# One DMA queue with a four-slot ring, and output weights cut by partitions, in a cached-attention decode kernel

## The chip, the core and the metric

The kernel runs on one core of one Trainium2 chip. The metric is the device time of one execution in microseconds (us), measured on the chip. The core has five engines with instruction streams of their own: TensorE (PE), VectorE (DVE), ScalarE (ACT), GpSimd (POOL) and SyncE (SP). Transfers from memory to the on-chip buffer (128 partitions) are issued by SP or ACT, each into its own hardware queue, and are carried out by 16 DMA engines that both queues share.

## What is computed

One decode step for four sequences: layer norm, attention over a cache, output projection and residual, then layer norm, a gated block and a second residual.

```python
def _A_ref(x, k_cache, v_cache, wq, wo):          # B=4, Sq=1, D=512, H=32, Sk=8192, Dh=128
    q = (x @ wq).reshape(B, Sq, H, Dh).transpose(0, 2, 1, 3)
    scores = jnp.einsum("bhqd,bhkd->bhqk", q, k_cache) * (Dh ** -0.5)
    p = _softmax(scores, axis=-1)
    o = jnp.einsum("bhqk,bhkd->bhqd", p, v_cache)
    return o.transpose(0, 2, 1, 3).reshape(B, Sq, H * Dh) @ wo

def _B_ref(x, w_gate, w_up, w_down):              # F=1792
    g = jnp.einsum("bsd,df->bsf", x, w_gate)
    u = jnp.einsum("bsd,df->bsf", x, w_up)
    return jnp.einsum("bsf,fd->bsd", _sigmoid(g) * u, w_down)

h  = x + _A_ref(_layernorm(x), k_cache, v_cache, wq, wo)
h2 = h + _B_ref(_layernorm(h), w_gate, w_up, w_down)
```

All data are bf16. The two caches are 268 MB each, so nearly everything that the kernel reads is keys and values.

## The kernel before

**Tiles.** The 128 pairs of sequence and head are the steps s. Two heads make one tile t of 4 MB: `ring[:, slot, :]`, 128 partitions with 32 KB each. There are 64 key tiles and 64 value tiles. The ring has NS = 4 slots. `place` (L179 to L189) gives the slots: key tile t has slot t % 2, value tile t has slot 2 + t % 2. The query weights (`wq`) begin in slot 3, and slot 2 first holds the re-ordered queries ("qr"). After the attention slot 0 takes the gate and up weights, slot 1 the down weights.

**A step.** VectorE transposes half a key tile into `kT` with four instructions (L389), TensorE multiplies it by the queries (L407). Every eight steps (GS = 8, a group) the maximum is taken (L445 to L462), ScalarE applies the exponential (L466, L468), the probabilities are transposed (L484) and copied (L498). LAG = 10 steps after its scores a step's values are used (`pe_pv`, L431): in program order TensorE runs score(s), then P·V(s − 10). Each group of results is scaled (L503), transposed (L510) and kept in `OT` (L515).

**What sets the order of loads.** `P(engine, ...)` appends an instruction to that engine's list; each engine works its list in order, and an instruction with dependencies makes its engine wait. Loads are such instructions. SP issues wq, all 64 key tiles, then gate, up and down weights (L251, L252). ACT issues x (L202), value tiles 0 and 1 once the queries are in place (L521, L522), and each further value tile t in the main loop, right after the P·V that uses up tile t − 2, between its own exponentials and copies. A load waits until the tile that was in its slot is used up: for keys its last transpose, for values its last P·V (`consumed`). Gate, up and down weights wait also for P·V of step 123 (`pv_of[NST - 5]`).

**Output weights.** `wo` (4 MB, 32 heads × 128 rows × 512) lands in the space of `kT`, so its loads wait for the last score (`sc_of[NST - 1]`). They are eight transfers of all 128 partitions × 4 heads, 512 KB each, in contiguous pieces of 1 KB (L209), issued by ACT between the value tiles 61, 62 and 63 (`wo_after`). The last value tile comes in three pieces (`VL_PARTS`, L217), the down weights in three parts (`WD_PARTS`, L225).

**The end.** After all output weights have landed TensorE multiplies those of 24 heads (L578), then the P·V of the last value tile follows piece by piece, its scaling, the output projection's rest (L578), the residual and layer norm (L598 to L615), gate and up (L624), sigmoid and product (L629, L630), down (L638), the second residual (L644), a transposition (L647, L649) and the store (L653).

## Time and profile before

| | us |
|---|---|
| three timed runs | 1314.25, 1317.78 (median), 1319.87 |
| the profiled execution | 1314.25 |
| its span, first to last instruction | 1312.3 |
| VectorE busy | 625.6 (48%) |
| TensorE matmuls busy | 473.4 (36%) |
| ScalarE busy | 46.0 (4%) |
| SP's queue (q1) | 278.14 MB, 49.6% of 16 engines' time |
| ACT's queue (q10) | 272.64 MB, 48.7% |
| key tile, issue to landing | 29.6 |
| value tile, issue to landing | 32.2 |
| one part of the output weights | 18.8 |

A row of groups on the page gives line, engine and operation, output from input, shape and count, then busy time, mean duration in ns, idle time of that engine just before them and what ended it. The chain of waits follows the work that ended last back to its releaser at each step; in it "ACTq L209" is time in which ACT's sequencer was busy issuing the DMA of line 209. Slices are fortieths of the span, 32.8 us each. Windows are stretches of our choice with the busy time of every engine.

The packet records behind the page list every packet of every DMA with its queue, size, start and duration. Their medians are: 32 KB (one partition of a key or value tile) 1215 ns, 16 KB 618 ns, 8 KB 315 ns, 3.5 KB (gate and up weights) 147 ns, 1 KB (output and down weights) 47 ns. Each transfer of 128 partitions also has 16 packets of 4 B, its completions.

### The profile page before, as it was taken

To read this page: it belongs to the slowest core of one execution; us is meant where nothing else is said; L and a number is where in the kernel's file an instruction comes from. 1 tells how busy PE (TensorE), PEld (TensorE's weight loads), DVE (VectorE), ACT (ScalarE), POOL (GpSimd) and SP (SyncE) were. 2 spreads that over 40 slices of the span, in tenths; PEclk is the share of its full clock that TensorE was granted. 3 is DMA by queue.
4 is the path that set the end of the run, shared out by engine and by line. 5 is a ranking of instruction groups with operands and counts; after the bars stand their busy time and mean duration, and the time that the engine had idled before them with its cause. 6 is when DMAs were issued, how large, how long until landed. Compare 5 with 4: busy or idle time off the path is not lost.

```text
span 1312.3 us, 12694 instructions
## 1 busy us (share of the span) xinstructions
PE 473.4 (36%) x5827; PEld 176.8 (13%) x5827; DVE 625.6 (48%) x641; ACT 46.0 (4%) x102; POOL 10.6 (1%) x22
## 2 busy tenths in 40 slices
PE   2134342333333253332334244243243234323324
PEld 1011110111111010110111011011111111111113
DVE  5486455445355355445446445445535436545300
ACT  2000000000000000000000000000000000000000
POOL 3000000000000000000000000000000000000000
PEclk9997556775566656676665655676556665577665
DMA  9999999999999999999999999999999999999895
GB/s 402 432 380 418 434 430 432 430 431 429 430 432 430 431 430 432 431 430 431 429 431 432 431 431 432 431 430 432 428 432 431 430 430 431 431 430 430 356 396 209
DMA packets 26076, 551.58 MB, mean 420 GB/s; under 512 B 2340, under 2 KB 8232, under 8 KB 9256
## 3 DMA queue, kind: packets, MB, share of 16 engines
q1 hardware_dynamic: 12288, 278.14, 49.6%
q10 hardware_dynamic: 13736, 272.64, 48.7%
q8 instruction: 45, 0.74, 0.2%
q14 instruction: 7, 0.06, 0.0%
HBM read 550.77 MB, written 0.00 MB: 420 GB/s over the span
## 4 chain that ended last, share of the span: by engine, by line
DMA 71%; DVE 24%; ACTq 3%; PE 1%; issue 1%; ACT 0%; DVEq 0%
DMA ring<-in_A_k_cache_dram 66%; DVE kT L389 22%; DMA ring<-in_A_v_cache_dram 3%; ACTq L209 2%; DMA ring<-in_A_wq_dram 1%; ACTq L217 1%; DVE mx L445 1%; ACTq L245 0%; PE PS L322 0%; DVE Lq L366 0%; DVE rowx L457 0%; PE PS L624 0%; PE PS L431 0%; DVE mrow L455 0%; DVE ring L339 0%
## 5 line engine op out<-in xcount | busy, mean ns | idle before, releaser
L389 DVE STREAM_TRANSPOSE kT<-ring 128x1024 uint32<-128x1024 uint32 x512 | 588.2, 1209 | 591.1 <-DMA ring<-in_A_k_cache_dram 591.1
L407 PE MATMUL PS<-kT,Lq 128*32 128x512 bf16 x2048 | 217.6, 566 | 773.5 <-DVE kT L389 606.5
L431 PE MATMUL PS<-ring,PTz 128*32 128x512 bf16 x2048 | 210.1, 553 | 33.9 <-DMA ring<-in_A_v_cache_dram 33.6
L407 PEld LDWEIGHTS PS<-kT,Lq 128*32 128x32 bf16 x2048 | 53.9, 119 | 914.8 <-DVE kT L389 673.0
L431 PEld LDWEIGHTS PS<-ring,PTz 128*32 128x32 bf16 x2048 | 64.8, 125 | 132.8 <-issue 81.0
L466 ACT ACTIVATE negm<-PS 128x1 f32<-128x1 f32 x16 | 2.7, 171 | 1157.2 <-PE PS L462 1157.2
L503 DVE TENSOR_SCALAR Zs<-PS,rinv 128x512 f32<-128x512 f32 x16 | 11.6, 724 | 49.4 <-PE PS L431 49.4
L498 ACT ACTIVATE PTz<-PS 64x512 bf16<-64x512 f32 x32 | 18.9, 591 | 18.5 <-PE PS L484 18.1
L510 PE MATMUL PS<-SelZ,Zs 128*128 128x8 f32 x128 | 18.2, 269 | 0.9 <-DVE Zs L503 0.9
L510 PEld LDWEIGHTS PS<-SelZ,Zs 128*128 128x128 f32 x128 | 16.7, 204 | 10.2 <-issue 8.4
L484 PEld LDWEIGHTS PS<-Sel,E_sb 128*32 128x32 bf16 x1024 | 11.3, 100 | 9.1 <-ACT E_sb L468 6.7
L484 PE MATMUL PS<-Sel,E_sb 128*32 128x32 bf16 x1024 | 11.4, 188 | 1.5 <-ACT E_sb L468 1.1
L445 DVE TENSOR_REDUCE mx<-PS 128x1 f32<-128x512 f32 x16 | 10.5, 657 | 1.3 <-PE PS L407 1.2
L468 ACT ACTIVATE E_sb<-PS,negm 128x512 bf16<-128x512 f32 x16 | 11.0, 687 | 0.5
L473 PEld LDWEIGHTS PS<-sig,Gsum 128*128 128x128 f32 x32 | 7.8, 305 | 12.6 <-issue 12.6
L515 DVE CAST OT<-PS 128x8 bf16<-128x8 f32 x16 | 2.1, 132 | 15.5 <-PE PS L510 15.5
L473 PE MATMUL PS<-sig,Gsum 128*128 128x1 f32 x32 | 9.2, 356 | 0.0
L578 PE MATMUL PS<-OT,kT 128*128 128x4 bf16 (+2 forms) x160 | 4.6, 167 | 11.3 <-DMA kT<-in_A_wo_dram 11.0
L462 PE MATMUL PS<-onesf,rowx 1*128 1x1 f32 x32 | 7.5, 300 | 0.0
L462 PEld LDWEIGHTS PS<-onesf,rowx 1*128 1x128 f32 x32 | 6.1, 237 | 9.8 <-issue 9.8
L339 DVE CAST ring<-PS 128x512 bf16<-128x512 f32 x4 | 2.5, 684 | 9.8 <-PE PS L322 9.8
L578 PEld LDWEIGHTS PS<-OT,kT 128*128 128x128 bf16 x160 | 4.4, 103 | 12.2 <-issue 11.9
(78 smaller groups left out, 77.1 us busy)
## 6 DMA issues: line engine op xcount, KB each, us to landing
ring<-in_A_k_cache_dram SPq DMA_DIRECT2D x64, 4096.0 KB, 29.6
ring<-in_A_v_cache_dram ACTq DMA_DIRECT2D x63, 4096.0 KB, 32.2
ring<-in_A_wq_dram SPq DMA_DIRECT2D x1, 4096.0 KB, 12.2
kT<-in_A_wo_dram ACTq DMA_DIRECT2D x8, 512.0 KB, 18.8
ring<-in_A_v_cache_dram ACTq DMA_DIRECT2D x1, 2048.0 KB, 28.3
ring<-in_A_v_cache_dram ACTq DMA_DIRECT2D x2, 1024.0 KB, 21.8
ring<-in_B_w_gate_dram SPq DMA_DIRECT2D x1, 1792.0 KB, 16.2
ring<-in_B_w_up_dram SPq DMA_DIRECT2D x1, 1792.0 KB, 21.8
```

The lines of the kernel that those rows point to most:

```text
L209: return [(lambda e: e.dma_start(wo_v[:, HW * t:HW * t + HW, :], A_wo.rearrange("(h p) f -> p h f", p=128)[:, HW * t:HW * t + HW, :]).then ...
L217: return e.dma_start(ringv(slot)[:, c0:c1], kv_src(t, A_v_cache)[:, c0:c1]).then_inc(s_piece[i], 16)
L389: return e.transpose(kT[:, buf, i * q:(i + 1) * q].bitcast(U32), ringv(src)[:, base + i * q:base + (i + 1) * q].bitcast(U32))
L407: mm = e.matmul(bS[g % 2][32 * j:32 * (j + 1), :], Lq[:, l0:l0 + 32], rhs, start=(s % GS == 0 and v == 0), stop=(s % GS == GS - 1 and v == 3),
L431: mm = e.matmul(bO[g % 2][32 * rq:32 * (rq + 1), :], PTz[:, g % 2, l0:l0 + 32], ringv(slot)[:, r0 * 128:(r0 + 4) * 128], start=(s % GS == ...
L445: mx_of[g] = P("dve", lambda e: e.tensor_reduce(mx[:, :], bS[g % 2][:, :], AX.X, ALU.max), [sc_of[g * GS + GS - 1], p1_of.get(g - 1)])
L462: p2_of[g] = P("pe", lambda e: e.matmul(bX[:, 0:1], rowx[0:1, :], onesf[0:1, 0:1], start=True, stop=True), [d2b_of[g], c_ones])
L473: L_of[g] = P("pe", lambda e: e.matmul(bX[:, 0:1], Gsum[:, :], sig[:, 0:1], start=True, stop=True), [exp_of[g], a1_of[g], d_g])
L484: mm = e.matmul(bP[g % 2][32 * a:32 * (a + 1), 32 * rr:32 * rr + 32], E_sb[:, 32 * rr:32 * rr + 32], Sel[:, a, :], start=True, stop=True, ...
L498: return e.activation(dst, src, ACT.Copy)
L503: z_of[g] = P("dve", lambda e: e.tensor_scalar(Zs[:, :], bO[g % 2][:, :], rinv[:, g % 2:g % 2 + 1], None, op0=ALU.mult), [pv_of[g * GS + G ...
L510: mm = e.matmul(bX[:, 256:264], Zs[:, 128 * r:128 * (r + 1)], SelZ[:, r, :], start=(r == 0), stop=(r == 3))
```

## The change

All loads but that of x are issued by SP, in one order: wq, key tiles 0 to 4, then alternately key t and value t − 5, the last five value tiles, and gate, up and down weights. The four slots are given in turn to every load in that order, instead of two to keys and two to values. The output weights stand after value 60 (two transfers), after value 61 (five) and after value 62 (three). They are ten transfers instead of eight: four of partitions 0 to 79 with eight heads each (640 KB), and six of eight partitions each (80 to 87, and so on to 127) with all 32 heads (256 KB). All still wait for the last score. The extra wait of gate, up and down weights goes. The compute instructions and their order stay, except that "qr" moves from slot 2 to slot 3.

```diff
-        NWO = 8
-        HW = H // NWO
...
-        place(("wq", 0), 3)
-        for t in range(NT2):
-            place(("k", t), t % 2)
-            place(("v", t), 2 + t % 2)
-        place(("wg", 0), 0)
-        slot_of[("wu", 0)], prev_of[("wu", 0)] = 0, prev_of[("wg", 0)]
-        place(("wd", 0), 1)
+        WO_PARTS = [(0, 80, 8 * i, 8 * i + 8) for i in range(4)] + [(p, p + 8, 0, H) for p in range(80, 128, 8)]
+        NWO = len(WO_PARTS)
+        LAG2 = LAG // 2
+        items = [("wq", 0)]
+        for t in range(NT2 + LAG2):
+            if t < NT2:
+                items.append(("k", t))
+            if t >= LAG2:
+                items.append(("v", t - LAG2))
+            for i in {LAG2 - 4: (0, 1), LAG2 - 3: (2, 3, 4, 5, 6), LAG2 - 2: (7, 8, 9)}.get(t - NT2, ()):
+                items.append(("wo", i))
+        items += [("wg", 0), ("wu", 0), ("wd", 0)]
+        slot_of, prev_of, dma_of = {}, {}, {}
+        owner = [None] * (NS - 1) + [("qr", 0)]
+        uses = [0] * NS
+        cur = 0
+        for it in items:
+            if it[0] == "wo":
+                continue
+            if it[0] == "wu":
+                slot_of[it], prev_of[it] = slot_of[("wg", 0)], prev_of[("wg", 0)]
+                continue
+            slot_of[it] = cur
+            prev_of[it] = [owner[cur]] if owner[cur] is not None else []
+            owner[cur] = it
+            cur = (cur + 1) % NS
...
             if kind == "wo":
+                p0, p1, h0, h1 = WO_PARTS[t]
                 return [(lambda e: e.dma_start(
-                    wo_v[:, HW * t:HW * t + HW, :],
-                    A_wo.rearrange("(h p) f -> p h f", p=128)[:, HW * t:HW * t + HW, :]).then_inc(s_wo, 16),
+                    wo_v[p0:p1, h0:h1, :],
+                    A_wo.rearrange("(h p) f -> p h f", p=128)[p0:p1, h0:h1, :]).then_inc(s_wo, 16),
                     s_wo, 16 * NWO)]
...
-        for it in [("wq", 0)] + [("k", t) for t in range(NT2)] + [("wg", 0), ("wu", 0), ("wd", 0)]:
-            issue("sp", it)
+        for it in items:
+            dma_of[it] = [P("sp", fn, (), sem, val) for fn, sem, val in load(it)]
...
-        issue("act", ("v", 0))
-        issue("act", ("v", 1))
-        wo_after = {NT2 - 3: (0, 1), NT2 - 2: (2, 3, 4), NT2 - 1: (5, 6, 7)}
...
-            t = (s - LAG - 1) // 2 + 2
-            if (s - LAG) % 2 == 1 and 2 <= t < NT2:
-                for i in wo_after.get(t, ()):
-                    issue("act", ("wo", i))
-                issue("act", ("v", t))
...
-        for it, ops in dma_of.items():
-            for op in ops:
+        for it in items:
+            for op in dma_of[it]:
                 op.deps = [sc_of[NST - 1]] if it[0] == "wo" else [consumed[p] for p in prev_of[it]]
-                if it[0] in ("wg", "wu", "wd"):
-                    op.deps.append(pv_of[NST - 5])
```

## Prediction

> **What bounds the kernel now.** I read the page's slices first, then the DMA windows where the slices dip, then the chain of waits at the end.

> ```profile
> span 1312.3 us, 12694 instructions
> ...
> DMA  9999999999999999999999999999999999999895
> GB/s 402 432 380 418 434 430 432 430 431 429 430 432 430 431 430 432 431 430 431 429 431 432 431 431 432 431 430 432 428 432 431 430 430 431 431 430 430 356 396 209
> DMA packets 26076, 551.58 MB, mean 420 GB/s; under 512 B 2340, under 2 KB 8232, under 8 KB 9256
> ```

> From slice 4 to 36 the rate sits at 428 to 434 GB/s with the DMA engines busy throughout, while VectorE, the busiest compute engine, works 48% of the span. The middle is bound by bytes. In the timeline the first transposes of successive key tiles start at 1140.73, 1160.16, 1179.59 and 1199.01: 19.43 us for one key and one value tile, so 9.715 us per 4 MB tile. Only the dips can be won: slices 2, 3 and the last three.

> The windows of 10 us over the first dip (columns: busy time of each engine, clock, DMA share, GB/s):

> ```profile
> 80.00:90.00 10.00, 4.10 (x33) 0.98 (x33) 9.40 (x10) 0.00 (x0) 0.00 (x0) 1.00 0.86 338
> 90.00:100.00 10.00, 4.55 (x98) 2.00 (x98) 8.69 (x10) 2.13 (x5) 0.00 (x0) 1.00 0.91 367
> 100.00:110.00 10.00, 5.36 (x58) 1.83 (x50) 7.00 (x8) 0.00 (x0) 0.00 (x0) 0.89 0.98 398
> ```

> Here both value slots are full and the values' use begins ten half-tiles after the keys' (LAG). Only keys flow, through two slots; the next load waits for eight transposes (9.13 us), and DMA runs dry in between. Against 432 the five windows from 60 to 110 lose 5.4 us.

> The last lines of the chain of waits (start, length, what):

> ```profile
> 1262.66 10.18 ACTq L217
> 1272.84 0.03 issue
> 1272.87 1.41 ACTq L217
> 1274.28 0.03 issue
> 1274.31 22.60 DMA ring<-in_A_v_cache_dram
> 1296.92 0.04 issue
> 1296.96 1.07 PE PS L431 x5
> ```

> The last value pieces are issued late from ACT, behind the output weights, and land while gate, up and down weights arrive on the other queue. After 1296.96 DMA has nothing left and 15.3 us of compute follow alone. A third hole is around 1220 to 1240: value tile 60 is issued at 1229.9, when tile 58 has been used, and the two windows there run at 234 and 389 GB/s, 5.6 us lost.

> **The change, part by part.**

> *One queue, four slots in turn.* Sixty-four key loads, all value loads and the output weights now stand on SP in one order. Is one queue as fast as two? From 10 to 20 us, before the first value is issued (22.57), SP's queue alone moved 436 GB/s, and the packet records show ACT's alone at 432 GB/s from 1246 to 1252. So no loss per tile; bound 0 to 0.03 us, over 125 tiles under 4 us.

> SP now stops at each slot wait and everything behind it stops too. A load waits for the use of the tile four loads earlier. A key tile is used up 9.13 to 10.6 us after landing; three more tiles (29.1 us) stand between it and its successor, so 18 us stay queued. A value tile is used about 5 us after landing (score, 1.9 us, and P·V, 1.9 us, twice, behind the key's second half), leaving 24 us. The tightest spots: key 2 waits for the query transposition (done at 21.15; key 1 keeps DMA busy to 32), the first value behind key 5 waits for key 2's transposes (53; DMA is busy to 71). Output weights wait for the last score, some 3 us after value 58 lands, with values 59 and 60 (19 us) queued. All hidden; if a cover failed, the cost is one issue-to-data gap of about 2 us.

> ACT loses 74 issues. Its longest wait row, 1157.2 us for the max, is slack, so this is worth nothing by itself.

> The start is no longer starved: keys 0 to 5 flow at 9.715 us each, transposes with their chain steps need about 10 us, three slots of lead take the difference. The first tile (query weights) lands at 12.9 as now. Then 64 keys and values 0 to 60 are 125 tiles × 9.715 = 1214.4, so value 60 lands at 1227.3.

> *The end.* Behind it in the same queue: values 61 to 63, 3 × 9.715 = 29.1; output weights 4096 packets of 1 KB at 47 ns over 16 engines, 12.0; gate and up 1024 × 147 ns / 16 = 9.4; down 1792 × 47 ns / 16 = 5.3. DMA would end at 1283.1 if all were spread evenly. The last values now land 14.7 us before that end. From there to the normalized row is 7.5 us (1296.96 to 1304.42), gate/up 3.2, sigmoid and product 0.3: 11.0, beside the remaining 14.7, with 3.7 us of cover. What stays after DMA is landing 0.3, the last two sevenths of L638 (1.67 → 0.5) and from its end 1309.65 to 1312.3, 2.65. Together 3.4 and **1286.5**: 25.8 below now. The places seen add up to 5.4 + 5.6 + (15.3 − 3.4) = 22.9; 3 us of that gain I cannot place.

> *The output weights' new shapes.* Four transfers of 80 rows × 8 heads, then six of 8 rows × 32 heads. How many engines take a transfer is visible in the small packets: 146 transfers, 145 of them with 16 completion packets make 2320, the result's 16 pieces of 256 B make 2336, and the 2340 of the page leave 4 for the load of x, which has four rows. Transfers of 80 = 16 × 5 rows should then use 16 engines, 4 × 40 × 47 ns = 7.5 us. An 8-row transfer should use 8, each with 32 packets: the loads of the other 8 engines do not help. Engines drain in order, so the loaded half ends last, and everything after it in its queue is late.

> Its price c is not in the trace. Lower end: eight engines run free of each other, 32 × 47 ns = 1.5 us; the nearest row is x, whose four packets to four neighbouring partitions took 44, 44, 44 and (the first) 506 ns, two of them at the same time. Upper end: eight partitions take no more than the one engine that feeds eight partitions of every 4 MB tile, 256 KB in 9.7 us. On the same grounds the 80-row transfers cost up to 2.4 us in place of 1.9, 2.2 in all. The end is at 1286.5 − 12.0 + 7.5 + 6c = **1282.0 + 6c**: 1291.0 at the lower end, 1340.2 at the upper. x is one packet per engine and shows no sustained rate; the tile shows one, but never several engines upon the same partitions. Neither is like 32 packets from each of eight engines, so I take the middle, c = 5.6, and 1315.6.

> [...]

> *Scale.* The profiled execution took 1314.25 for a span of 1312.3, 1.95 around it; the median of the three runs, 1317.78, is 3.5 above it. I add both: 1315.6 + 5.5 = **1321**.

> **The rivals.** A measurement of this kernel can tell about 0.5%, 6.6 us, from no change; the limits are 1311.2 and 1324.4. By 1282.0 + 6c they lie at c = 3.95 and 6.15, and the balance at 5.05.

> 1. Forecast: the gain of one full queue is eaten by the eight-row transfers, c about 5.6 (4.0 to 6.1): 1311 to 1324. Chance 0.42.
> 2. The eight engines do not hinder each other, or the transfers are spread over all 16 and so do nothing: 1296.5, or 1292 when even. For it: x's overlapping packets, and that the hole-free queue is then all that counts. Against: x is 4 KB. With prices between, up to c = 3.9: 1292 to 1311. Chance 0.28.
> 3. Slower: eight neighbouring partitions are fed at little more than one engine's 27 GB/s, from c = 6.15 on, up to 1345.7. For it: no eight partitions are ever filled faster in the trace. Against: that rate is the engine's own, 32 KB in 1.215 us. Value 62's load, which stands between the two groups of three, then competes for the same partitions and lengthens both. Chance 0.25.
> 4. The one queue stalls at a slot: if each of 64 pairs lost 0.5 us (the 60 to 110 stretch lost 5.4 us on some four keys), 32 us, 1353 with c = 5.6. The backlog of 18 us speaks against it. Chance 0.05.

> **How the numbers follow.** Faster is case 2, 0.28; within 0.5% is case 1, 0.42; slower is 3 and 4, 0.30. The likeliest is 1321, its own range 1311 to 1324. For 8 in 10 I go from 1293, taking in case 2 nearly whole, to 1337, which is c = 8.25; beyond that I leave about 0.1, and 0.03 below.

> **What would show it.** Right on the queue: slices 2 and 3 at 428 or more, one hardware queue with nearly all the packets, pairs still 19.43 us apart, value 60 landing near 1227. Right on the end: the last load to land is the down weights', some 3.4 us before the end. Right on c: between the landing of value 61 and the first part of value 63 the rate falls to about half or less for some 30 us, and the six transfers take about 34 us of it. The forecast is wrong if that stretch stays above 300 GB/s (case 2), if it lasts over 37 us (case 3), or if SP's waits show DMA idle in the middle (case 4).

## The result, and the profile after

The changed kernel takes 1332.19 us (median of four runs, 1329.23 to 1333.36) against 1316.43 for the kernel before: ratio 1.0114, 95% interval 1.0085 to 1.0143. It is slower by about 1.1%. The profiled execution took 1332.54 for a span of 1330.8. The forecast of 1321 had it unchanged; the range of 1293 to 1337 held it.

From the page of the changed kernel, the span, the DMA rows of the 40 slices (33.3 us each), the queues and the chain:

```profile
span 1330.8 us, 12695 instructions
...
DMA  9999999999999999999999999999999999999987
GB/s 409 425 436 429 431 433 427 434 430 430 431 429 435 429 431 428 431 435 428 432 431 428 436 426 431 433 429 436 427 430 434 427 433 431 430 434 399 226 192 272
...
q1 hardware_dynamic: 26000, 550.78, 98.9%
...
DMA 82%; PE 12%; SPq 3%; DVE 3%; issue 0%
```

The dip in slices 2 and 3 is gone: 436 and 429 where 380 and 418 stood. One queue carries 550.78 MB at the same rate as two did (426 to 436 GB/s in slices 2 to 35, 428 to 434 in slices 4 to 36 before). The loss is at the other end: the last three slices at 226, 192 and 272 GB/s, although the DMA engines still count as nine, eight and seven tenths busy in them. For much of that time bytes move slowly (233 GB/s at a share of 1.03 from 1240 to 1250); engines are not simply without work.

The bytes moved tell how far the queue's gain went. By the packet records 63.62 MB have been moved by 150 us (61.46 before) and 516.08 MB by 1200 us (513.94 before): a lead of some 2.15 MB, 5.0 us at 431 GB/s, won in slices 2 and 3 and kept to the last keys. The keys' own lead is larger (key tile 8 starts at 130.82 in place of 143.87, key 63 at 1205.75 in place of 1218.43), but the rest of it is order: the new order loads fewer values ahead of a key, and they are left over for the end. So the change wins 5.0 us at the start; with a span 18.5 us longer it loses 23.5 at the end.

The windows of the changed kernel after key 63 (busy times, clock, DMA share, GB/s):

```profile
1220.00:1230.00 10.00, 6.06 (x55) 2.12 (x51) 1.19 (x3) 0.95 (x3) 0.00 (x0) 0.67 1.02 355
1230.00:1240.00 10.00, 1.51 (x74) 1.15 (x62) 0.81 (x2) 2.67 (x4) 0.00 (x0) 0.50 1.04 277
1240.00:1250.00 10.00, 5.42 (x40) 3.06 (x40) 0.17 (x1) 0.00 (x0) 0.00 (x0) 0.50 1.03 233
1250.00:1260.00 10.00, 0.00 (x0) 0.00 (x0) 0.00 (x0) 0.00 (x0) 0.00 (x0) 0.50 0.83 202
1260.00:1270.00 10.00, 3.60 (x32) 1.09 (x32) 0.00 (x0) 0.00 (x0) 0.00 (x0) 0.66 1.03 152
1270.00:1280.00 10.00, 0.00 (x0) 0.00 (x0) 0.00 (x0) 0.00 (x0) 0.00 (x0) 0.51 0.98 275
1280.00:1290.00 10.00, 0.00 (x0) 0.00 (x0) 0.00 (x0) 0.00 (x0) 0.00 (x0) 0.50 0.56 153
1290.00:1300.00 10.00, 3.60 (x32) 1.08 (x32) 0.00 (x0) 0.00 (x0) 0.00 (x0) 0.50 0.93 182
1300.00:1310.00 10.00, 4.17 (x132) 3.62 (x133) 0.00 (x0) 0.00 (x0) 0.00 (x0) 0.50 0.99 390
```

Seventy microseconds, from 1230 to 1300, run below 300 GB/s. Two kinds of loss can be read apart. From 1230 to 1250 the DMA share is over 1.0 and the rate 277 and 233 GB/s: packets take longer. The packet records say the same: 32 KB packets that start after 1226 have a median of 1849 ns (1215 before), 1 KB packets of the output weights 95 ns (47 before). From 1280 to 1290 the share is 0.56: half of the engines have nothing to do.

Why they have nothing shows in SP's timeline of the changed kernel (start, duration, issue):

```profile
1221.25 0.51 SPq L258 DMA_DIRECT2D ring<-in_A_v_cache_dram  x1
1221.81 41.74 SPq L222 DMA_DIRECT2D kT<-in_A_wo_dram  x5
1263.59 2.96 SPq L258 DMA_DIRECT2D ring<-in_A_v_cache_dram  x1
1266.59 23.33 SPq L222 DMA_DIRECT2D kT<-in_A_wo_dram  x3
1289.96 2.14 SPq L230 DMA_DIRECT2D ring<-in_A_v_cache_dram  x3
```

SP is held for 41.74 us in five output-weight issues, and value 62, next in its order, goes out only at 1263.59. No new tile can start until then; the DMA share falls to 0.83 from 1250 to 1260 and, in the second hold, to 0.56 from 1280 to 1290. Being held is not new with these cuts: in the kernel even_parts below, which has 128-row transfers in the same places, SP's timeline shows

```profile
1221.59 22.79 SPq L222 DMA_DIRECT2D kT<-in_A_wo_dram  x3
```

and value 62 goes out there at 1244.43. What differs is how long the hold lasts.

The chain's end in the changed kernel is as forecast, the down weights last and 3.4 us behind them:

```profile
1310.73 16.69 DMA ring<-in_B_w_down_dram
1327.42 0.05 issue
1327.47 0.60 PE PS L639 x16
```

### The profile page after: what moved, and what is told of

It is laid out like the page before. It is cut to its first block, busy times and chain, and to the rows that moved or that the text cites. A ratio compares the mean times of both kernels' runs of the same rounds, so it can differ in the third digit from the quotient of the medians.

```text
span 1330.8 us, 12695 instructions
## 1 busy us (share of the span) xinstructions
PE 502.1 (38%) x5827; PEld 193.5 (15%) x5827; DVE 625.4 (47%) x641; ACT 46.0 (3%) x102; POOL 10.6 (1%) x22
## 2 busy tenths in 40 slices
DMA packets 26060, 551.58 MB, mean 414 GB/s; under 512 B 2324, under 2 KB 8216, under 8 KB 9240
## 3 DMA queue, kind: packets, MB, share of 16 engines
q1 hardware_dynamic: 26000, 550.78, 98.9%
## 4 chain that ended last, share of the span: by engine, by line
DMA 82%; PE 12%; SPq 3%; DVE 3%; issue 0%
DMA ring<-in_A_v_cache_dram 80%; PE PS L441 7%; PE PS L417 4%; DVE kT L399 2%; SPq L222 2%; DMA ring<-in_B_w_down_dram 1%; SPq L238 1%; DMA ring<-in_A_wq_dram 1%; SPq L258 0%; PE PS L332 0%; DVE Lq L376 0%; SPq L230 0%; DVE ring L349 0%; PE PS L359 0%; PE PS L639 0%
## 5 line engine op out<-in xcount | busy, mean ns | idle before, releaser
L417 PE MATMUL PS<-kT,Lq 128*32 128x512 bf16 x2048 | 242.0, 620 | 561.2 <-DVE kT L399 442.9
L441 PE MATMUL PS<-ring,PTz 128*32 128x512 bf16 x2048 | 217.3, 570 | 240.8 <-DMA ring<-in_A_v_cache_dram 239.9
L417 PEld LDWEIGHTS PS<-kT,Lq 128*32 128x32 bf16 x2048 | 69.1, 136 | 691.6 <-DVE kT L399 472.1
L520 PE MATMUL PS<-SelZ,Zs 128*128 128x8 f32 x128 | 19.2, 277 | 0.9 <-DVE Zs L513 0.9
L472 PEld LDWEIGHTS PS<-onesf,rowx 1*128 1x128 f32 x32 | 6.7, 261 | 12.5 <-issue 12.5
```

Of the source, the lines that this page charges most:

```text
L417: mm = e.matmul(bS[g % 2][32 * j:32 * (j + 1), :], Lq[:, l0:l0 + 32], rhs, start=(s % GS == 0 and v == 0), stop=(s % GS == GS - 1 and v == 3),
L441: mm = e.matmul(bO[g % 2][32 * rq:32 * (rq + 1), :], PTz[:, g % 2, l0:l0 + 32], ringv(slot)[:, r0 * 128:(r0 + 4) * 128], start=(s % GS == ...
L472: p2_of[g] = P("pe", lambda e: e.matmul(bX[:, 0:1], rowx[0:1, :], onesf[0:1, 0:1], start=True, stop=True), [d2b_of[g], c_ones])
L520: mm = e.matmul(bX[:, 256:264], Zs[:, 128 * r:128 * (r + 1)], SelZ[:, r, :], start=(r == 0), stop=(r == 3))
```

## The experiments

The theories: **N**, engines that write neighbouring partitions at the same time hinder each other; **M**, wider, any cut of fewer than 128 rows hinders, because its rows are handed to other engines than in a 128-row tile, so that engines out of step meet; **Q**, the one queue itself costs; **S**, the source rows are slow; **B**, the loss is the engine time while SP is held. Spans of profiled executions are compared unless a ratio is given; 1312.3 is the kernel before, 1330.8 the changed one. Executions of one kernel differ, by 0.4 us in even_parts, by about 1 us in the two kernels with eight-row cuts only and by some 5 us in the kernel before, so smaller differences of spans mean little. "..." in an edit marks lines left out. Where the number of transfers changes, so does the line that places them in the order (two after value 60, the others after 61 and 62); it is shown once, for even_parts.

### Even parts: the queue without the new cuts

```diff
-        WO_PARTS = [(0, 80, 8 * i, 8 * i + 8) for i in range(4)] + [(p, p + 8, 0, H) for p in range(80, 128, 8)]
+        WO_PARTS = [(0, 128, 4 * i, 4 * i + 4) for i in range(8)]
...
-            for i in {LAG2 - 4: (0, 1), LAG2 - 3: (2, 3, 4, 5, 6), LAG2 - 2: (7, 8, 9)}.get(t - NT2, ()):
+            for i in {LAG2 - 4: (0, 1), LAG2 - 3: (2, 3, 4), LAG2 - 2: (5, 6, 7)}.get(t - NT2, ()):
```

> The changed kernel with the output weights cut as before: eight transfers of all 128 partitions x 4 heads, two after value 60, three after 61, three after 62. Theory N (engines that write neighbouring partitions at the same time hinder each other): the whole loss lies in the shapes, so what stays is the full queue: the prediction's 1286.5, plus 64 x 0.1 us because the mean pair of tiles took 19.54 and not 19.43, gives a span of 1293 and a time of about 1295, some 1.7% under the kernel before. Theory Q (the loss lies in the one queue, whose waits block everything behind them): the span stays over 1315, however the weights are cut.

Measured: 1296.49 us, ratio to the kernel before 0.9854 (0.9838 to 0.9871), span 1294.8. This version beats both kernels. Two rows of its page and the same stage of its windows:

```profile
span 1294.8 us, 12693 instructions
...
GB/s 405 435 428 431 435 427 431 433 430 431 431 432 430 433 430 429 433 430 430 434 429 430 434 428 431 434 428 433 432 428 433 430 430 432 432 431 431 427 378 317
```

```profile
1230.00:1240.00 10.00, 4.84 (x103) 2.37 (x96) 0.82 (x2) 2.67 (x4) 0.00 (x0) 0.67 1.01 406
1240.00:1250.00 10.00, 2.29 (x24) 1.41 (x27) 0.17 (x1) 0.00 (x0) 0.00 (x0) 0.67 0.86 320
1250.00:1260.00 10.00, 2.34 (x24) 0.64 (x16) 0.00 (x0) 0.00 (x0) 0.00 (x0) 0.50 1.02 420
1260.00:1270.00 10.00, 6.25 (x131) 3.79 (x132) 0.00 (x0) 0.00 (x0) 0.00 (x0) 0.50 1.02 390
```

Theory Q falls. One queue with four slots is worth −17.5 us of span (19.1 us by the medians), of which 5.0 come at the start and 12.5 at the end, and the cuts alone cost 1330.8 − 1294.8 = 36.0. What the one order, the shared slots and the missing extra wait give singly no run shows.

### Half of the weights in eight-row cuts, neighbouring or four apart

```diff
+        WO_PARTS = [(0, 64, 8 * i, 8 * i + 8) for i in range(4)] + [(p, p + 8, 0, H) for p in range(64, 128, 8)]   # half_adjacent
...
+        WO_PARTS = [(0, 64, 8 * i, 8 * i + 8, 1) for i in range(4)] + [(p, p + 29, 0, H, 4)
+                                                                     for p in (64, 65, 66, 67, 96, 97, 98, 99)]    # half_spaced
...
+                    wo_v[p0:p1:ps, h0:h1, :],
+                    A_wo.rearrange("(h p) f -> p h f", p=128)[p0:p1:ps, h0:h1, :]).then_inc(s_wo, 16),
```

> Changed kernel with half of the output weights in eight-row transfers of neighbouring partitions (64 to 71, and so on to 127), the other half in four transfers of partitions 0 to 63 x 8 heads. Eight transfers of the disputed kind in place of six. Theory N with the price that the changed kernel shows (about 7 us each): 1293 - 12 + 4 x 1.5 to 2.4 + 8 x 7 = 1343 to 1347 of span. Theory E (the price is only that eight of 16 engines carry them, 1.5 us each): 1293 - 12 + 6 + 12 = 1299. Theory S (the eight engines are slowed at the source, where they read neighbouring 1 KB rows with the same large stride): 1343 to 1347 as well.

> The same as the kernel half_adjacent, but the eight rows of a transfer are four apart (64, 68, ... 92; then 65, 69, ...; and so on up to 99, 103, ... 127). Bytes, packets, count of transfers, engines and order are the same. Theory N: the partitions are no longer neighbours, each transfer costs about 1.5 us, the span is 1299 to 1303, and 1 KB packets of this stage take about 47 ns again. Theory E, or that SP's blocked issue is what costs: no difference from half_adjacent. Theory S: faster too, since the source rows are four apart as well; the next kernel tells N and S apart. [...]

Measured: neighbouring 1330.78 us (ratio 1.0116, 1.0095 to 1.0136), span 1329.3; four apart 1321.17 us (1.004, 1.0024 to 1.0056), span 1319.5. Both figures missed all that was written down: the first is 14 us or more under theory N's, the second 16 or more over it. Two things follow. The spacing is worth 9.8 us, so neighbours do matter. But eight cuts cost no more than the change's six, and with neighbours gone 24.7 us over even_parts remain: the eight-row cuts are not the whole, and what else is new here are the wide cuts, 64 rows here, 80 in the change. The records show it in the tiles: 32 KB packets that start after 1226 keep a median of 1599 ns in half_spaced.

### The same destinations, other source rows

```diff
+        WO_PARTS = [(0, 64, 8 * i, 8 * i + 8, 0, 64, 1) for i in range(4)] + [(64 + 8 * i, 72 + 8 * i, 0, H, p, p + 29, 4)
+                                                                            for i, p in enumerate((64, 65, 66, 67, 96, 97, 98, 99))]
...
+                    wo_v[p0:p1, h0:h1, :],
+                    A_wo.rearrange("(h p) f -> p h f", p=128)[q0:q1:qs, h0:h1, :]).then_inc(s_wo, 16),   # q: the rows four apart
```

> Written to neighbouring partitions as in half_adjacent, but read from the rows four apart that half_spaced reads. The rows of half of the output weights land in other partitions than the product needs, so this kernel computes another projection; its work and its times are otherwise those of half_adjacent. Theory N (destination): slow, 1343 to 1347 of span, within 5 us of half_adjacent. Theory S (source): fast, 1299 to 1303, like half_spaced.

Measured: 1334.08 us (ratio 1.0141, 1.0114 to 1.0167), span 1329.8, against 1329.3 for half_adjacent and the 1299 to 1303 that theory S expected. Which rows are read makes no difference that these runs can tell; which are written does. Theory S falls.

### Wide cuts only

```diff
+        WO_PARTS = [(0, 80, 8 * i, 8 * i + 8) for i in range(4)] + [(80, 128, 8 * i, 8 * i + 8) for i in range(4)]
```

> Changed kernel without eight-row transfers: four of partitions 0 to 79 x 8 heads as in it, and four of partitions 80 to 127 x 8 heads (48 rows, three for each of 16 engines). Theory E8 (the eight-row transfers are the cost, as the prediction's 6c has it; the 80-row ones cost at most 2.2 us): span 1295 to 1299 against 1294.8 of even_parts. Theory M (every transfer of fewer than 128 rows costs, since its rows go to engines that are not the ones which fill those partitions in the value tiles, so that engines out of step meet on the same partitions): over 1308, because value 61 landed 13.7 us late in the changed kernel with nothing but two 80-row transfers ahead of it and two behind it; 32 KB packets of this stage would take up to 2 us in place of 1.2, as in the changed kernel.

Measured: 1320.65 us (ratio 1.0035, 1.0022 to 1.0048), span 1318.2: 23.4 over even_parts, with no eight-row cut at all and, by the author's estimate (80 = 16 × 5 rows, 48 = 16 × 3), all 16 engines in every transfer. 32 KB packets that start after 1226 have a median of 1635 ns. That is what theory M expected. The prediction had put the 80-row cuts at 2.2 us at most; the 23.4 hold four 48-row cuts too, and no run parts the two.

### Eight-row cuts only

```diff
+        WO_PARTS = [(0, 128, 4 * i, 4 * i + 4) for i in range(5)] + [(p, p + 8, 20, H) for p in range(0, 128, 8)]   # rows8_adjacent
...
+        WO_PARTS = [(0, 128, 4 * i, 4 * i + 4, 1) for i in range(5)] + [(32 * g + i, 32 * g + i + 29, 20, H, 4)
+                                                                      for g in range(4) for i in range(4)]          # rows8_spaced
```

> Changed kernel without 80-row transfers: 20 heads by five transfers of all 128 partitions x 4 heads, the other 12 heads (three eighths, as in the change) by sixteen transfers of eight neighbouring partitions x 12 heads, 96 KB each. Engines alone (eight of 16 carry 16 x 12 packets of 47 ns, 9.0 us in place of 4.5): 1294.8 + 4.5 = 1299. With packets of about 100 ns, as in the changed kernel: 19.2 in place of 4.5, 1309 to 1315 with the meeting of value tiles added. If 80-row transfers were the whole loss: 1299.

> As rows8_adjacent, but the eight rows of each transfer are four apart. If neighbouring partitions are what hinders the eight engines: about 1299, 10 us or more under rows8_adjacent, with 1 KB packets near 47 ns. If the transfers' count or the eight engines alone matter: the same as rows8_adjacent.

Measured: neighbouring 1309.18 us (ratio 0.9946, 0.9927 to 0.9965), span 1307.7, 12.9 over even_parts; four apart 1302.38 us (0.9898, 0.987 to 0.9926), span 1301.1, 6.3 over it. The same three eighths of the weights as in the change go in transfers of eight rows. Of 12.9 us, 6.6 go with the neighbours, less than the 10 that were expected; the 6.3 that stay are near the estimate of 4.5 that eight engines cost by doing the work of sixteen (counted as in the prediction, the changed kernel's 2324 packets under 512 B agree with eight completions for each of its eight-row cuts and 16 for each 80-row one). With the rows four apart the tiles keep their pace (32 KB packets after 1226: median 1214 ns, one in ten over 1244). With neighbours the median is 1218, but it hides the packets beside the cuts: the 39 that start between 1250 and 1260 have a median of 1736 ns.

Where each kernel's stage falls back shows in the starts of the P·V that wait for values 60, 61, 62 and the last piece of 63:

| | value 60 | 61 | 62 | last of 63 | span |
|---|---|---|---|---|---|
| even_parts | 1236.23 | 1248.73 | 1262.87 | 1277.16 | 1294.8 |
| rows8_spaced | 1236.47 | 1249.14 | 1266.94 | 1284.15 | 1301.1 |
| rows8_adjacent | 1236.34 | 1249.53 | 1273.60 | 1290.73 | 1307.7 |
| rows80_rows48 | 1241.80 | 1264.32 | 1287.66 | 1301.29 | 1318.2 |
| the changed kernel | 1240.84 | 1262.48 | 1296.01 | 1313.83 | 1330.8 |

Value 61 is 13.7 us late in the changed kernel, with 80-row cuts on both sides of it, and 15.6 us in rows80_rows48, where no eight-row cut follows. Even value 60, which stands ahead of every cut in the queue, is 4.6 us late. A reason that fits is that engines that finish their part of it first begin the cuts and write into partitions that the others are still filling; the packet records hold no engine numbers, so this is argued and not shown.

### The cuts in the kernel with two queues

The kernel before with the new `WO_PARTS`, and `wo_after = {NT2 - 3: (0, 1), NT2 - 2: (2, 3, 4, 5, 6), NT2 - 1: (7, 8, 9)}`.

> The kernel before, two queues and two slots each, with only the ten new cuts of the output weights, issued by ACT where it issued the eight. If the cuts cost by themselves, wherever they are queued: about 36 us more than the kernel before, as from even_parts to the changed kernel, a span near 1348. If it takes the one queue, in which the rest of the loads stand behind blocked issues: clearly less, under 1325, since gate, up and down weights flow on SP meanwhile.

Measured: 1349.67 us (ratio 1.0258, 1.0229 to 1.0287), span 1347.3, 35.0 over the kernel before (33.5 by the medians). The cuts cost about the same under two queues as under one. Here too the values land late, the last piece at 1331.9 in place of 1296.9.

### Cuts away from the tiles

```diff
-            for i in {LAG2 - 4: (0, 1), LAG2 - 3: (2, 3, 4, 5, 6), LAG2 - 2: (7, 8, 9)}.get(t - NT2, ()):
-                items.append(("wo", i))
-        items += [("wg", 0), ("wu", 0), ("wd", 0)]
+        items += [("wg", 0), ("wu", 0), ("wd", 0)] + [("wo", i) for i in range(NWO)]
```

In even_cuts_last `WO_PARTS` is that of even_parts, in new_cuts_last that of the change.

> even_parts with all eight 128-row transfers of the output weights moved behind the down weights, the last loads of the queue. They then run with no value tile near them. The product with the output weights, the last values' product and all that follows (3.6 + 3.6 + 14.2 us by the rows of the kernel before) come after DMA's end: span about 1291 + 21 to 22 = 1313. A control for the next kernel; 12 us for the eight transfers.

> The changed kernel with its ten transfers (four of 80 rows, six of eight neighbouring rows) moved behind the down weights, so that they meet no value tile. If most of the 36 us came from meeting the value tiles (engines out of step writing the partitions that another engine fills): the four 80-row transfers take 8 to 10 us, 1 KB packets at 47 to 60 ns, and only the eight-row ones stay dear (32 packets of 80 to 100 ns, 2.6 to 3.2 us each): 24 to 29 us in all, 12 to 17 over even_cuts_last. If the shapes cost as much by themselves: 30 us or more over it.

Measured: with eight even parts last 1313.37 us (ratio 0.9984, 0.9973 to 0.9996), span 1312.2, as expected. With the ten cuts last 1334.77 us (1.0137, 1.0046 to 1.0228), span 1330.2. The cuts by themselves cost 18.0 by the spans and 21.4 by the medians, between the two expectations; new_cuts_last has only two executions, 5.4 us apart. The windows of new_cuts_last at its end, when all value tiles have landed (the last down weights land at 1282.82, the 80-row cuts come before the eight-row ones):

```profile
1275.00:1280.00 5.00, 0.00 (x0) 0.00 (x0) 0.00 (x0) 0.00 (x0) 0.00 (x0) 0.50 1.03 224
1280.00:1285.00 5.00, 0.00 (x0) 0.00 (x0) 0.00 (x0) 0.00 (x0) 0.00 (x0) 0.50 1.12 189
1285.00:1290.00 5.00, 0.00 (x0) 0.00 (x0) 0.00 (x0) 0.00 (x0) 0.00 (x0) 0.50 1.06 170
1290.00:1295.00 5.00, 0.00 (x0) 0.00 (x0) 0.00 (x0) 0.00 (x0) 0.00 (x0) 0.50 0.84 100
1295.00:1300.00 5.00, 0.00 (x0) 0.00 (x0) 0.00 (x0) 0.00 (x0) 0.00 (x0) 0.50 0.58 89
1300.00:1305.00 5.00, 0.00 (x0) 0.00 (x0) 0.00 (x0) 0.00 (x0) 0.00 (x0) 0.50 0.55 99
```

and of even_cuts_last, whose last down weights land at 1279.02:

```profile
1275.00:1280.00 5.00, 0.00 (x0) 0.00 (x0) 0.00 (x0) 0.00 (x0) 0.00 (x0) 0.50 0.98 316
1280.00:1285.00 5.00, 0.00 (x0) 0.00 (x0) 0.00 (x0) 0.00 (x0) 0.00 (x0) 0.50 1.10 351
```

With no tile near, the stretch that holds the 80-row cuts runs at 224 to 170 GB/s with all engines counted busy, where 128-row parts run at 316 to 351 (no window holds 80-row cuts alone: the first two still hold down weights, the third the first eight-row cuts). From 1295 on the eight-row cuts run at 89 to 99 GB/s on a DMA share of a good half. At that rate 256 KB is 2.6 to 2.9 us.

So about half of the 36.0 us (18.0 by the spans) is the cuts' own pace, and the other half arises only when they stand among the value tiles.

### Every second row

```diff
+        WO_PARTS = [(p, 8 * i, 8 * i + 8) for i in range(4) for p in range(2)]
...
+                    wo_v[p0::2, h0:h1, :],
```

> even_parts with eight transfers of 64 rows, every second partition (0, 2, ... 126; then 1, 3, ... 127) x 8 heads, in place of eight of 128 rows x 4 heads. Same bytes, packets, engines and places in the queue. If a transfer of fewer than 128 rows is dear in itself, or if its rows go to other engines than in a 128-row tile: like rows80_rows48, 1310 or more, with 32 KB packets over 1.3 us. If 128-row tiles give eight consecutive rows to each engine, these transfers give each engine four of its own eight, nobody meets, and the span stays at 1295. [...]

Measured: 1296.44 us (ratio 0.9846, 0.9804 to 0.9888), span 1294.5: as even_parts, with 32 KB packets at 1216 ns. A transfer of 64 rows is not dear in itself, so theory M does not hold for every cut of fewer than 128 rows. Rows spread evenly over all 128 partitions are harmless here (span 1294.5 against 1294.8); the same number crowded into one half is not, as far as half_spaced tells (1319.5), where eight-row cuts four apart stand beside such wide cuts. The span is the one that the expectation gave for engines that each keep to their own eight rows of a tile. The packet records hold no engine numbers, so that is argued and not shown.

### The cuts on the other queue

In the changed kernel the loads of "wo" leave SP's order and are issued by ACT in the main loop:

```diff
...
+            t = (s - LAG - 1) // 2 + 2
+            if (s - LAG) % 2 == 1:
+                for i in {NT2 - 3: (0, 1), NT2 - 2: (2, 3, 4, 5, 6), NT2 - 1: (7, 8, 9)}.get(t, ()):
+                    dma_of[("wo", i)] = [P("act", fn, (), sem, val) for fn, sem, val in load(("wo", i))]
```

> The changed kernel with its ten cuts of the output weights issued by ACT, on the second hardware queue, after the exponentials of the last group; all other loads stay on SP's queue, which then has no output weights in it. Theory B (part of the 36 us is engine time lost while SP is held at a full queue and the idle half of the engines gets no value tile; by the packet records some 7 us of all 16 engines between 1226 and 1292): the span falls by 5 to 10, to 1321 to 1326. Theory M (engines that write the same partitions at the same time are the whole of it): no gain, 1329 or more, and up to 1345 since cuts and tiles now meet for longer.

Measured: 1336.55 us (ratio 1.0158, 1.0141 to 1.0175), span 1334.9. The number is theory M's, but not for its reason. The last loads, now the output weights, land here before the first product with them:

```profile
1314.34 3.55 PE L581 MATMUL PS<-OT,kT 128*128 128x4 bf16 x128 [52.64 <-DMA kT<-in_A_wo_dram]
```

In the changed kernel the last load lands at 1327.42. So DMA as a whole ends 13 us earlier here. The span does not fall because the output weights now come last, and 20.6 us of compute stand behind them instead of 3.4. That DMA ends earlier does not speak for theory B. Only 491 of the 4096 packets of output weights start before 1260, and the last 32 KB packet ends at 1257.4: the cuts ran mostly after the tiles and hardly met them, though theory M's expectation had them meet for longer. 32 KB packets after 1226 have a median of 1285 ns.

**Slow packets or idle engines.** The packet records can part the two. From 1226 us to the last landing, this is the time that passed, the durations of all packets in it divided by 16 engines, and what is left, the time that an engine stood without a packet (in the changed kernel up to 22 packets are under way at once on the 16 engines, so packets of one engine can overlap a little, and it is a rough figure):

| us | time | packets | of them value tiles (32 and 16 KB) | of them 1 KB pieces | without a packet |
|---|---|---|---|---|---|
| even_parts | 65.4 | 62.5 | 29.3 | 18.2 | 2.9 |
| rows8_spaced | 71.3 | 64.3 | 30.6 | 18.6 | 7.0 |
| rows8_adjacent | 77.8 | 70.3 | 32.9 | 22.1 | 7.5 |
| rows80_rows48 | 88.3 | 83.5 | 40.1 | 28.0 | 4.8 |
| the changed kernel | 101.4 | 91.1 | 44.5 | 31.4 | 10.3 |
| even_cuts_last | 64.6 | 62.1 | 28.4 | 18.6 | 2.5 |
| new_cuts_last | 83.6 | 74.7 | 28.5 | 31.1 | 8.9 |
| new_cuts_on_act | 88.2 | 79.0 | 30.4 | 29.5 | 9.2 |

Of the changed kernel's 36.0 us over even_parts, 28.6 are packets that last longer (15.2 of the value tiles, 13.2 of the 1 KB pieces) and 7.4 are engines without one. With the cuts last, the 1 KB pieces lose nearly as much (12.5) and the tiles nothing. So what arises only among the tiles is the tiles' own slow packets. Moving the cuts to ACT takes 14.1 us from the tiles' packets and 1.1 from the engines' empty time: theory B, as far as this run tells, is worth little.

## Why the prediction was right or wrong

**The queue: right.** One queue ran at 426 to 436 GB/s from slice 2 to slice 35, no slot wait let DMA run dry in the middle, slices 2 and 3 filled, and the down weights landed last, 3.4 us before the end. With even parts the sum of 1286.5 met a span of 1294.8, and value 60, forecast to land near 1227, is used from 1236.23. Of the 8.3 us, about 7 are the term "19.43 us" for a pair of tiles: it was read from three periods in a row, and the mean over keys 8 to 63 is 19.54 in both kernels (1074.6 us over 55 pairs before, 1074.9 after), 0.11 more for each of 64 pairs; 1.3 stay unplaced. By place, the start gave 5.0 us for the 5.4 forecast, the end 12.5 for the 17.5 (5.6 + 11.9).

**The cuts: right in kind, wrong in place and size.** The step that failed is "1282.0 + 6c". It charged 29.1 us to the six eight-row transfers at c = 5.6 and allowed the 80-row ones 2.2 us at most. Measured, the cuts cost 36.0, so with the pair's mean put right c would be (1330.8 − 1289) / 6 = 7.0, beyond the 6.15 where rival 3 began. But c is no property of those six: eight-row cuts alone cost 12.9 (rows8_adjacent), and wide cuts alone 23.4, with none of eight rows. In the changed kernel itself the window from 1230 to 1240 is down to 277 GB/s (even_parts: 406), and SP's first eight-row issue starts only at 1241.16. Counting 16 engines for 80 rows and concluding that they were nearly free was the error; what mattered was which partitions were written, and that the value tiles' packets slowed with them (32 KB at a median of 1635 ns in rows80_rows48, 1216 with every second row).

**The number: in part luck.** The span came 15.2 us over the forecast 1315.6, 8.3 from the queue and 6.9 from the cuts; the scale (5.5 us added, 1.4 found) gave 4.1 back, so the median came 11 over 1321. The range held it with a width that was meant for the price of six cuts, while much of the cost came from the other four and from the tiles.

**The bounds.** The lower end, eight engines free of each other, is nearly what spaced rows show (6.3 us in place of 4.5). The upper end, 9.7 us for each eight-row cut, is reached in no run that shows their pace: 2.6 to 2.9 alone. The single row of the load of x, two overlapping packets to neighbouring partitions at 44 ns, told nothing of sustained writing; to weigh it lightly was right.

**The rivals.** Rival 3 came nearest, with its chance of 0.25: slower, by how fast a block of partitions is filled, and value tiles drawn into it. Its place was wrong in the same way. Rival 4 did not happen as it was put, a slot that stalls; the queue did hold SP, for 41.74 and 23.33 us, in the cuts' own issues, which the prediction mentioned as engines draining in order and did not price. Even parts hold it too, for 22.79 and 6.83.

**The sign looked for.** "About half or less for some 30 us", and over 37 us for case 3: the stretch under 300 GB/s lasts 70. It was looked for after value 61 (used from 1262.48); it began at 1230.

What stays open is why packets to a block of partitions last longer: because engines meet on the same partitions, or because a part of the partitions takes only part of the rate. No run shows either. Cuts of 64 contiguous rows by themselves were not run either.

## What to carry to other kernels

When the middle of a kernel is bound by bytes, look at what fills the DMA engines in the first and last per cent: one queue in order of use, with slots shared by all loads, was worth 1.5% here (all three together), with no compute changed. Cut a transfer along the free dimension and keep all 128 partitions in it (or rows spread evenly over them); a cut by blocks of partitions lost its own rate here (170 to 224 GB/s where 128-row parts ran at 316 to 351) and slowed the full tiles beside it (32 KB packets at 1849 ns for 1215). And a mean rate should be taken over the whole stage: three clean periods understated this one by 0.11 us in 19.54, about 7 us in all.
